# Row maxima on ScalarE's queue and GpSimd, both banks of the v sums copied at once, and low parts listed first

## The chip, the cores and the metric

One core of a Trainium2 chip runs the whole kernel. Its engines are TensorE (PE, with its weight loads shown apart as PEld), VectorE (DVE), ScalarE (ACT), GpSimd (POOL) and SyncE (SP), which in this kernel issues nearly all DMAs. The metric is the device time of one execution in microseconds. Before the change it is 772.84 us, the median of three runs (771.87 to 775.53).

## The reference

Two branches are computed from x (2048 rows of 512) and mixed by a gate:

```python
a  = x @ dft_hid_re.T ; b = x @ dft_hid_im.T
y  = dft_seq_re @ a - dft_seq_im @ b          # Fourier branch
q, k, v = split(x2 @ wqkv)                    # 32 heads of 16
p  = softmax(mask(q @ k.T / 4))               # keys i-255 .. i only
o  = (p @ v) @ wo                             # attention branch
g  = sigmoid(sum(x * gate_w))
out = g * y + (1 - g) * o
```

## The kernel before

**Precision.** Products that need it are made in two parts: an operand becomes a high part (a cast by `hi_of`, L103, on ACT) and a low part (raw minus high, `lo_of`, L106, on DVE or POOL), and three matmuls (high-high, high-low, low-high; `TERMS`) are summed.

**Attention.** 32 heads stand in eight groups of four, each with 16 blocks of 128 rows; the loop at the end of the program walks over the 128 blocks n. For a block, `s_head` (L442) multiplies queries by keys into a PSUM bank, and DVE (L445) finds each row's maximum into a column of `nm`, negated and masked. Nine blocks later (`LAG`), `t_head` (L497) makes the same scores transposed, with the maximum as two more rows of the contraction (the high and low part of it), and ACT takes the exponential (L498) into `pt`. POOL blanks the corners of the window (`t_mask`, L504 and L508). After four blocks `pv` (L523) multiplies `pt` by v into two banks `ot`, one for each half of the contraction.

**How the maxima get there.** Once per four blocks `m_rows` (L449) splits `nm` into two parts and transposes them on DVE (L452, L453, L455), writes them to DRAM (`m_scr<-mt`), and reads them back into rows 48 and 49 of `ring` (`ring<-m_scr`). Below such a round is called a batch; there are 33. `t_head` of three blocks later needs them.

**Banks.** The scores s, the transposed scores t and the two sums o take turns in four PSUM banks (`ps_a`, tag "st"). PE cannot start the next one before the oldest bank has been read: an s bank by DVE, a t bank by ACT, the o banks by ACT's copy (L529) and DVE's sum (L530).

**The other work.** `dense` is a generator of matmuls that the loop calls in between (`fill`): first the projections (to about 320 us), then 32 `c_block`s of the sequence DFT. Each of these takes a piece of the DFT matrix, loaded as `raw` and `big` tiles, split by `piece_split`: the high part, three plus or minus operations on the other quarters (L328, L331, on POOL twice and DVE once), the low part, and sums of magnitudes on ACT (L566), which a final guard adds up. When the loop is over, the rest of the `c_block`s and the output product (`wo_run`) follow.

**What sets the order.** Nothing schedules by itself: each engine runs its instructions in the order in which the program issues them, and waits in line. `defer(t, f)` issues f after t ticks; every matmul of `dense` is a tick, a step of the attention loop (one of the four heads of a block) is 0.7 and calls 2.8 of these matmuls in the first stretch and 1.25 in the second, and a `pv` is followed by `tick(9)` at once. So all that falls due in those nine ticks is issued just behind the `pv`. A DMA is issued by an engine too (`ld` takes SP), and an engine that must wait before it issues one holds up what stands behind it.

Of the kernel before, what the change touches and what calls it, by code (L numbers as in the profile page):

```python
# [8 lines left out]
F32 = mybir.dt.float32  # L9
# [41 lines left out]
def fnet_window_mix(ctx: ExitStack, tc: tile.TileContext, xT, x, wqk, wv, wr, wi, cr, ci, wo, gw, out):  # L51
# [44 lines left out]
    def ld(dst, src):  # L96
        nc.sync.dma_start(dst, src)  # L97

    def f(ap):
        return ap.bitcast(F32)  # L100
# [348 lines left out]
    def m_rows(u):  # L449
        m = ML.pop(u)  # L450
        hl = at.tile([P, 2, 16], F32R, name="mhl", bufs=1)
        nc.vector.tensor_scalar(hl[:, 0], m, -1.0, None, op0=OP.mult)  # L452
        nc.vector.scalar_tensor_tensor(hl[:, 1], m, -1.0, f(hl[:, 0]), op0=OP.mult, op1=OP.subtract)  # L453
        mt = at.tile([P, 32], F32, name="mt", bufs=1)
        nc.vector.transpose(mt, f(hl[:]).rearrange("q l c -> q (l c)"))  # L455
        ms = m_scr[u + LAG // 4 + 1]

        def write():
            ld(ms.rearrange("l h p b i q -> i (l h p b) q"), mt)
            defer(12, read)  # L460

        def read():
            b, end = max(0, LAG + 4 * u), min(NS * NB, LAG + 4 * u + 4)
            while b < end:
                e = min(end, (b // NB + 1) * NB)
                o = b - LAG - 4 * u
                for h in range(2):
                    ld(f(ring[0][64 * h + 48:64 * h + 50, :, b % NB * P:b % NB * P + (e - b) * P]),
                       ms[:, h, :, o:o + e - b].rearrange("l p b i q -> l p (b i q)"))
                b = e  # L470
        defer(2, write)

    PT = {}
    VR = {}
# [36 lines left out]
    def pv(u, last=False):  # L511
        g, sb = divmod(u, 4)
        ot = [ps_a.tile([P, 512], F32, name="o", tag="st") for _ in range(2)]
        kbs = range(max(0, 4 * sb - 2), 4 * sb + 4)
        for kb in kbs:
            pt = PT[g * NB + kb]
            v2 = V2[g * 4 + kb // 4][:, kb % 4]
            for j in range(NH):
                for h in range(2):
                    r = slice(64 * h, 64 * h + 64)  # L520
                    a = max(kb * P + (64 * h if kb else 0), sb * 512)
                    e = min(kb * P + 64 * h + 320, sb * 512 + 512)
                    nc.tensor.matmul(ot[h][32 * j:32 * j + 32, a - sb * 512:e - sb * 512], v2[r, j],  # L523
                                     pt[r, j, a - kb * P:e - kb * P], start=kb == kbs[0], stop=kb == kbs[-1],
                                     skip_group_check=True)
            if kb < 4 * sb + 2 or sb == 3:
                PT.pop(g * NB + kb)
        os = at.tile([P, 512], F32, name="os", bufs=1)
        nc.scalar.copy(os, ot[0])  # L529
        defer(3, lambda: nc.vector.tensor_add(os, ot[1], os))  # L530
        hf = g // 4
        us, ls = u_scr[sb][hf], l_scr[sb][hf]
        d = 40

        def o_out():
            ld(us[g % 4].rearrange("j r s -> (j r) s"), os)
            if g % 4 == 3:
                defer(d, o_pack)

        def o_pack():  # L540
            rows_ = us.rearrange("g j r s -> (g j) r s")
            ld(ls[0], rows_[:, 16])
            ld(o_scr[sb][2 * hf:2 * hf + 2].rearrange("a (b d) s -> (a b) d s", d=16), rows_[:, 0:16])
            defer(d, l_in)

        def l_in():
            lt = at.tile([P, 64], F32, name="lt")
            ld(lt, ls[0].rearrange("j (a b) -> (j a) b", b=64))
            defer(d, l_inv, lt)

        def l_inv(lt):
            nc.vector.reciprocal(lt, lt)
            defer(4, l_back, lt)

        def l_back(lt):
            ld(ls[1].rearrange("j (a b) -> (j a) b", b=64), lt)
            have.add(("o", sb, hf))
        defer(7, o_out)

    order = [(i, 4 * m + c) for i in range(2) for c in CLASSES for m in range(4)]  # L560
    PIECE = {}
# [31 lines left out]
    def piece_split(n, at_=1, step=2):  # L593
        if n >= len(order):
            return
        i, tb = order[n]
        raws = PRAW.pop(n)
        main = raws[0][:, HALVES[0]]
        hi = ev.tile([P, 512], F32R, name="es", bufs=3)
        w = st.tile([P, 2, 512], F32R, name="hl")  # L600
        defer(at_, hi_of, hi, main)
        for k, j in enumerate((2, 1, 3)):
            d, src, sign = left(i, tb, raws, j)
            defer(at_ + step * k, minus if sign > 0 else plus, d, d, src, j != 3)
        defer(at_ + step * 3, lo_of, w[:, 0], main, hi, True)
        for k, d in enumerate((raws[0][:, HALVES[1]], raws[1])):
            defer(at_ + step * (5 + k), magnitudes, sums[:, 2 * n + k:2 * n + k + 1], d, d)
        if n % 16 == 0:
            defer(at_ + step * 4, magnitudes, gl[:, i:i + 1], main, main)
        PIECE[i, tb] = hi, w[:, 0]  # L610
        if n == len(order) - 1:
            defer(at_ + step * 8 + 10, guard)
# [408 lines left out]
```

## Time and profile before

| | us |
|---|---|
| median of three runs | 772.84 |
| the profiled execution | 772.52 |
| its span on the core | 770.8 |
| end of the projections, by the loads of the DFT pieces | about 320 |
| last exponentials of the attention loop | about 664 |

The program keeps three stretches apart: projections beside attention up to about 320 us, `c_block`s beside attention up to about 680 us, and the tail of output products. The profile's busy times are those of one execution. A row of the waits names the engine, tile and line that waited, what it waited for, and then the total in us, the number of times and the longest. A row of the timeline has the start, the length, the engine, line and operation, the tiles, the shapes and, in brackets, the idle time before and what ended it.

### The profile page before, as it was taken

How to read it: one execution, taken by the hardware profiler on the slowest of the kernel's cores; microseconds unless marked ns; L12 is line 12 of the kernel's file. 1: busy time of each engine (PE TensorE's matmuls, PEld its weight loads, DVE VectorE, ACT ScalarE, POOL GpSimd, SP SyncE). 2: the span in 40 equal slices, each digit the busy share in tenths (PEclk: the TensorE clock that was granted, in tenths of full speed). 3: DMA queues.
4: the chain of work that ended last, by engine and by line, in shares of the span. 5: the costliest groups of instructions: out<-in, count | busy, mean ns of one | idle time of the engine just before them, and what ended most of it. 6: DMA issues, size and time to landing. Idle time of an engine off the chain costs nothing.

```text
span 770.8 us, 18841 instructions
## 1 busy us (share of the span) xinstructions
PE 650.1 (84%) x6558; PEld 499.8 (65%) x6558; DVE 544.1 (71%) x1471; ACT 437.8 (57%) x928; POOL 470.4 (61%) x718
## 2 busy tenths in 40 slices
PE   9999999899999999978677978878887687835976
PEld 6788887777788777766455655655555456624754
DVE  5388878898897889768567757676678863516554
ACT  6334775455576545666577657656756567514230
POOL 5002565667667878787768859796875869822000
PEclk9999999999999999989789879978978868975979
DMA  7857775777666877798868678885877648697675
GB/s 281 264 171 221 221 233 174 214 215 219 212 206 194 236 211 216 251 277 251 254 182 248 220 203 248 263 247 148 269 205 242 209 162 301 233 297 259 189 249 155
DMA packets 99994, 174.36 MB, mean 226 GB/s; under 512 B 34420, under 2 KB 35316, under 8 KB 99764
## 3 DMA queue, kind: packets, MB, share of 16 engines
q1 hardware_dynamic: 98452, 170.98, 72.2%
q10 hardware_dynamic: 1440, 2.10, 0.8%
q8 instruction: 54, 0.88, 0.5%
q14 instruction: 48, 0.39, 0.2%
HBM read 114.03 MB, written 63.46 MB: 230 GB/s over the span
## 4 chain that ended last, share of the span: by engine, by line
DMA 18%; PE 17%; POOL 8%; DVE 8%; issue 6%; SPq 4%; ACT 3%; DVEq 0%; POOLq 0%; ACTq 0%
DMA ring<-m_scr 5%; PE d L238 5%; SPq L97 4%; PE t L234 4%; DVE sm L445 3%; PE o L523 3%; DMA raw<-cr 3%; DMA ring<-qk_scr 3%; PE t L497 2%; DMA pt<-o_scr 2%; PE s L442 2%; POOL pt L504 1%; POOL hl L106 1%; DMA hl<-cr 1%; DMA ev<-wo 1%
## 5 line engine op out<-in xcount | busy, mean ns | idle before, releaser
L445 DVE CUSTOM_DVE_ANT_0 sm<-s,mask 128x384 f32<-128x384 f32 (+2 forms) x512 | 269.8, 527 | 87.0 <-PE s L442 41.9
L498 ACT ACTIVATE pt<-t 128x384 f32<-128x384 f32 (+2 forms) x512 | 234.2, 475 | 131.8 <-PE t L497 93.7
L497 PE MATMUL t<-ring,ring 50*128 50x384 f32 (+2 forms) x512 | 199.9, 400 | 56.6 <-DMA ring<-m_scr 32.0
L442 PE MATMUL s<-ring,ring 48*128 48x384 f32 (+2 forms) x512 | 185.0, 372 | 24.2 <-DVE nm L445 22.5
L504 POOL TENSOR_SCALAR_AFFINE_SELECT pt<-pt 128x256 f32<-128x256 f32 x256 | 116.0, 454 | 124.2 <-ACT pt L498 117.0
L238 PE MATMUL d<-big,hl 64*128 64x512 f32 x896 | 171.8, 421 | 0.0
L497 PEld LDWEIGHTS t<-ring,ring 50*128 50x128 f32 x512 | 101.9, 202 | 89.0 <-issue 26.5
L442 PEld LDWEIGHTS s<-ring,ring 48*128 48x128 f32 x512 | 99.4, 198 | 78.7 <-DVE nm L445 66.3
L238 PE MATMUL d<-hl,big 64*128 64x512 f32 x984 | 147.9, 395 | 0.0
L238 PE MATMUL d<-big,es 64*128 64x512 f32 x448 | 122.7, 473 | 0.0
L238 PEld LDWEIGHTS d<-big,hl 64*128 64x128 f32 x896 | 110.0, 198 | 5.2 <-issue 0.6
L238 PEld LDWEIGHTS d<-hl,big 64*128 64x128 f32 x984 | 105.2, 186 | 6.9 <-issue 0.8
L508 POOL TENSOR_SCALAR_AFFINE_SELECT pt<-pt 128x256 f32<-128x256 f32 x224 | 95.3, 425 | 0.0
L523 PE MATMUL o<-pt,vpad 64*32 64x320 f32 (+5 forms) x2816 | 83.3, 373 | 5.9 <-DVE nm L445 3.7
L523 PEld LDWEIGHTS o<-pt,vpad 64*32 64x32 f32 x2816 | 66.6, 113 | 28.1 <-DVE nm L445 10.3
L238 PEld LDWEIGHTS d<-big,es 64*128 64x128 f32 x448 | 66.3, 224 | 2.5 <-issue 0.6
L106 POOL TENSOR_TENSOR hl<-es,hl 128x512 fp32r<-128x512 f32 x14 | 19.0, 1359 | 65.2 <-ACT hl L103 61.6
L529 ACT COPY os<-o 128x512 f32<-128x512 f32 x32 | 18.8, 587 | 64.2 <-PE o L523 64.2
L530 DVE TENSOR_TENSOR os<-o,os 128x512 f32<-128x512 f32 x32 | 22.1, 690 | 42.8 <-ACT os L529 38.8
L106 POOL TENSOR_TENSOR hl<-raw,es 128x512 fp32r<-128x512 f32 x32 | 44.0, 1375 | 0.0
L243 ACT ACTIVATE es<-d 128x512 f32<-128x512 f32 x53 | 31.7, 598 | 19.8 <-PE d L238 19.0
L106 POOL TENSOR_TENSOR big<-big 128x512 fp32r<-128x512 f32 x32 | 41.6, 1304 | 0.2 <-ACT big L103 0.2
(100 smaller groups left out, 902.5 us busy)
## 6 DMA issues: line engine op xcount, KB each, us to landing
qk_scr<-hl SPq DMA_DIRECT2D x32, 512.0 KB
ring<-qk_scr SPq DMA_DIRECT2D x128, 128.0 KB
ring<-qk_scr SPq DMA_DIRECT2D x128, 64.0 KB
u_scr<-os SPq DMA_DIRECT2D x32, 256.0 KB
raw<-cr SPq DMA_DIRECT2D x16, 512.0 KB
big<-cr SPq DMA_DIRECT2D x16, 512.0 KB
raw<-ci SPq DMA_DIRECT2D x16, 512.0 KB
big<-ci SPq DMA_DIRECT2D x16, 512.0 KB
```

Of the source, the lines that this page charges most:

```text
L97: nc.sync.dma_start(dst, src)
L106: (nc.gpsimd if pool else nc.vector).tensor_sub(lo, raw, f(hi))
L234: nc.tensor.matmul(pss[0], w, x, start=start, stop=stop)
L238: nc.tensor.matmul(pss[h], w[r], x[r], start=start, stop=stop)
L243: nc.scalar.activation(t, pss[0], AF.Copy, scale=scale)
L442: nc.tensor.matmul(ps[:, :w], ring[0][r, p, jb * P:(jb + 1) * P], ring[1][r, p, k0:k0 + w], start=True, stop=True)
L445: nc.vector.tensor_tensor_reduce(out=sm[:, :w], in0=ps[:, :w], in1=mask[:, WIN - w:], scale=1.0, scalar=3e38, op0=OP.add, op1=OP.min, accu ...
L497: nc.tensor.matmul(ps[:, :w], ring[1][r, p, q0:q0 + P], ring[0][r, p, q0:q0 + w], start=True, stop=True)
L498: nc.scalar.activation(pt[:, j, :w], ps[:, :w], AF.Exp, scale=-1.0)
L504: nc.gpsimd.affine_select(a, a, pattern=[[0, 2], [1, P]], compare_op=OP.is_ge, fill=0.0, base=0, channel_multiplier=-1)
L508: nc.gpsimd.affine_select(a, a, pattern=[[0, 2], [-1, P]], compare_op=OP.is_gt, fill=0.0, base=0, channel_multiplier=1)
L523: nc.tensor.matmul(ot[h][32 * j:32 * j + 32, a - sb * 512:e - sb * 512], v2[r, j], pt[r, j, a - kb * P:e - kb * P], start=kb == kbs[0], st ...
```

## The change

Four things are edited.

1. `m_rows`: the split of the maxima goes from two DVE instructions to three POOL instructions; the transpose stays on DVE, two ticks later; the write to DRAM and the reads back are issued by ACT instead of SP. The write is due 4 ticks after the split (2 before), the read 9 ticks after the write (12 before).
2. `pv`: DVE copies the second bank into a tile `o1` (one of the three "es" buffers) at once, and the sum is made by POOL three ticks later. The store of the sum is due after 12 ticks (7 before).
3. `piece_split`: the high part goes to the unused half of the tile that holds the low part, instead of an "es" buffer.
4. `piece_split`: the low part is due one step after the high part (three before), and the plus and minus operations two steps later than before. The sums of magnitudes keep their place.

```diff
-        nc.vector.tensor_scalar(hl[:, 0], m, -1.0, None, op0=OP.mult)
-        nc.vector.scalar_tensor_tensor(hl[:, 1], m, -1.0, f(hl[:, 0]), op0=OP.mult, op1=OP.subtract)
+        nc.gpsimd.tensor_scalar(hl[:, 0], m, -1.0, None, op0=OP.mult)
+        nc.gpsimd.tensor_add(m, m, f(hl[:, 0]))
+        nc.gpsimd.tensor_scalar(hl[:, 1], m, -1.0, None, op0=OP.mult)
...
-        nc.vector.transpose(mt, f(hl[:]).rearrange("q l c -> q (l c)"))
+        defer(2, nc.vector.transpose, mt, f(hl[:]).rearrange("q l c -> q (l c)"))
...
-            ld(ms.rearrange("l h p b i q -> i (l h p b) q"), mt)
-            defer(12, read)
+            nc.scalar.dma_start(ms.rearrange("l h p b i q -> i (l h p b) q"), mt)
+            defer(9, read)
...
-                    ld(f(ring[0][64 * h + 48:64 * h + 50, ...]), ...)
+                    nc.scalar.dma_start(f(ring[0][64 * h + 48:64 * h + 50, ...]), ...)
...
-        defer(2, write)
+        defer(4, write)
...
+        o1 = ev.tile([P, 512], F32, name="es", bufs=3)
         nc.scalar.copy(os, ot[0])
-        defer(3, lambda: nc.vector.tensor_add(os, ot[1], os))
+        nc.vector.tensor_copy(o1, ot[1])
+        defer(3, lambda: nc.gpsimd.tensor_add(os, o1, os))
...
-        defer(7, o_out)
+        defer(12, o_out)
...
-        hi = ev.tile([P, 512], F32R, name="es", bufs=3)
         w = st.tile([P, 2, 512], F32R, name="hl")
+        hi = w[:, 1]
...
-            defer(at_ + step * k, minus if sign > 0 else plus, d, d, src, j != 3)
-        defer(at_ + step * 3, lo_of, w[:, 0], main, hi, True)
+            defer(at_ + step * (k + 2), minus if sign > 0 else plus, d, d, src, j != 3)
+        defer(at_ + step, lo_of, w[:, 0], main, hi, True)
```

Because of added lines, what was L498 is L499 in the changed kernel, L529 is L531, and L566 is L569.

**The read of one batch, on SP and ACT.** The batch is the one whose write is issued at 371 us in the profile before (`m_scr_172`). On SP before, its write stands behind eight loads of the rings and two copies in DRAM, and its read behind the loads of a DFT piece (`raw<-cr`, `big<-cr`):

```order
L97 DMA ring_281<-qk_scr_2_3_105 16x2x512
L97 DMA l_scr_0_194<-u_scr_0_202 16x512
L97 DMA o_scr_208<-u_scr_0_202 16x8192
L97 DMA m_scr_172<-mt 4x32x32
L97 DMA r_scr_0_210<-ev 128x512
L97 DMA raw<-cr 128x1024
L97 DMA big<-cr 128x1024
L97 DMA u_scr_0_204<-os 128x512
L97 DMA vr<-v_scr_111 128x4x64
L97 DMA l_scr_0_192<-lt 128x64
L97 DMA ring_280<-m_scr_172 2x2x512 x2
```

On ACT in the changed kernel, behind the copy of the first bank of the same `pv` (`pt<-t` are the exponentials, `raw,sums` and `big,sums` the sums of magnitudes):

```order
L531 COPY os<-o 128x512
L460 DMA m_scr_172<-mt 4x32x32
L103 CAST big<-big 128x512
L569 ACTIVATE raw,sums<-raw 128x512
L499 ACTIVATE pt<-t 128x384
L103 CAST big<-big 128x512
L569 ACTIVATE big,sums<-big 128x1024
L499 ACTIVATE pt<-t 128x384 x3
L103 CAST big<-big 128x512
L499 ACTIVATE pt<-t 128x384
L469 DMA ring_280<-m_scr_172 2x2x512 x2
L499 ACTIVATE pt<-t 128x384 x3
```

The write has left SP's line for a place right behind the copy, and the read stands five exponentials further on.

**The two banks, on DVE.** At the same `pv`, before: the split and the transpose, a plus or minus of a DFT piece, and the sum of the banks:

```order
L452 TENSOR_SCALAR mhl<-nm 128x16
L453 SCALAR_TENSOR_TENSOR mhl<-nm,mhl 128x16
L455 STREAM_TRANSPOSE mt<-mhl 128x32
L328 TENSOR_TENSOR big<-big,raw 128x512
L530 TENSOR_TENSOR os<-o,os 128x512
L445 ISA sm,nm<-s,mask 128x384
```

and in the changed kernel:

```order
L532 COPY es<-o 128x512
L94 STREAM_TRANSPOSE mt<-mhl 128x32
L328 TENSOR_TENSOR big<-big,raw 128x512
L445 ISA sm,nm<-s,mask 128x384
L445 ISA nm 128x1
```

The copy comes first, the transpose behind it, and two instructions are gone from DVE.

**The last pieces, on POOL.** The end of POOL's program, where only DFT pieces are left, before (`hl<-raw,es` is the low part, `raw<-raw` and `big<-big,hl` the plus and minus operations):

```order
L331 TENSOR_TENSOR raw<-raw 128x512
L328 TENSOR_TENSOR big<-big,hl 128x512
L106 TENSOR_TENSOR hl<-raw,es 128x512
L331 TENSOR_TENSOR raw<-raw 128x512
L328 TENSOR_TENSOR big<-big,hl 128x512
L106 TENSOR_TENSOR hl<-raw,es 128x512
L618 MEMSET gl 128x1
```

and in the changed kernel, with a sum of the two banks ahead of them:

```order
L533 TENSOR_TENSOR os<-es,os 128x512
L106 TENSOR_TENSOR hl<-raw,hl 128x512
L331 TENSOR_TENSOR raw<-raw 128x512
L328 TENSOR_TENSOR big<-big,hl 128x512
L106 TENSOR_TENSOR hl<-raw,hl 128x512
L331 TENSOR_TENSOR raw<-raw 128x512
L328 TENSOR_TENSOR big<-big,hl 128x512
```

Each piece's low part now stands ahead of the other two instead of behind them.

More of the change, by code (lines that the diff above doesn't have):

```diff
@@ L467, in read @@
                 for h in range(2):
-                    ld(f(ring[0][64 * h + 48:64 * h + 50, :, b % NB * P:b % NB * P + (e - b) * P]),
-                       ms[:, h, :, o:o + e - b].rearrange("l p b i q -> l p (b i q)"))
+                    nc.scalar.dma_start(f(ring[0][64 * h + 48:64 * h + 50, :, b % NB * P:b % NB * P + (e - b) * P]),
+                                        ms[:, h, :, o:o + e - b].rearrange("l p b i q -> l p (b i q)"))
                 b = e
-        defer(2, write)
+        defer(4, write)
     PT = {}
```

## The prediction

> **What bounds the kernel now.** First the busy times by stage, each row with its length, the busy us of PE, PEld, DVE, ACT and POOL, the granted PE clock and the DMA share:
>
> ```profile
> 40.00:320.00 280.00, 265.72 (x3121) 222.73 (x3117) 241.76 (x721) 163.56 (x341) 176.49 (x288) 1.00 0.69 210
> 320.00:680.00 360.00, 283.22 (x3049) 201.93 (x3049) 240.88 (x655) 230.60 (x524) 274.38 (x412) 0.85 0.77 234
> ```
>
> Up to 320 us PE is idle for only 14 us of 280. From 320 to 680 us it is idle for 77 of 360 and its clock falls to 0.85: there is room there. Second, PE's own waits in that second stretch:
>
> ```profile
> PE t L497 <- DMA ring<-m_scr: 32.0, 12, 7.0
> PE s L442 <- DVE nm L445: 14.2, 16, 3.7
> PE t L497 <- ACT pt L498: 10.0, 15, 2.1
> PE t L497 <- DVE os L530: 4.8, 14, 1.0
> ```
>
> Half of the idle time named is twelve waits for maxima read back from DRAM. The chain of work that ended last says the same, by line:
>
> ```profile
> DMA ring<-m_scr 5%; PE d L238 5%; SPq L97 4%; PE t L234 4%; DVE sm L445 3%; PE o L523 3%; DMA raw<-cr 3%; DMA ring<-qk_scr 3%; PE t L497 2%; DMA pt<-o_scr 2%; PE s L442 2%; POOL pt L504 1%; POOL hl L106 1%; DMA hl<-cr 1%; DMA ev<-wo 1%
> ```
>
> These reads are its largest share. Third, one of the waits, in the timeline:
>
> ```profile
> 362.75 6.30 SPq L97 DMA_DIRECT2D ring<-qk_scr  x8
> 364.70 0.21 DVE L455 STREAM_TRANSPOSE mt<-mhl 128x32 f32<-128x32 f32 x1
> 365.94 0.59 ACT L529 COPY os<-o 128x512 f32<-128x512 f32 x1 [1.14 <-PE o L523]
> 366.56 0.69 DVE L530 TENSOR_TENSOR os<-o,os 128x512 f32<-128x512 f32 x1
> 371.27 0.56 SPq L97 DMA_DIRECT2D m_scr<-mt  x1
> 375.52 0.63 SPq L97 DMA_DIRECT2D ring<-m_scr  x2
> 380.66 0.66 PE L497 MATMUL t<-ring,ring 50*128 50x384 f32 x1 [7.01 <-DMA ring<-m_scr]
> ```
>
> The transpose was done at 364.9, its write left SP at 371.27, 6.4 us later, behind eight ring loads. The read left at 375.52, and 4.5 us after its last issue (376.15) PE went on.
>
> **The change part by part.** The sum is made against the profiled execution, 772.52 us (span 770.8 and 1.7 around it), 0.3 under the median.
>
> *Maxima on ACT's queue (gain 24, bounds 16 and 32).* The write now stands behind ACT's copy: in the batch above it could leave at about 367 instead of 371.27. The read stands nine ticks behind `pv`, half of the 18 to the product that needs it. There `pv` ended at 365.8 and PE wanted the maxima at 373.65 (380.66 less 7.01). Half of these 7.8 us and 0.7 for the copy ahead give 4.6, so the read leaves at 370.4. How fast it lands on ACT's queue no row shows. The nearest two are SP's: 4.5 us above, and
>
> ```profile
> 331.12 0.59 SPq L97 DMA_DIRECT2D m_scr<-mt  x1
> 333.97 1.55 SPq L97 DMA_DIRECT2D ring<-m_scr  x4
> 336.75 0.66 PE L497 MATMUL t<-ring,ring 50*128 50x384 f32 x1 [4.44 <-DMA ring<-m_scr]
> ```
>
> 1.2 us (from 335.52). With 1.2 us all waits go (32). With 4.5 us the same sum leaves 1.3 us of the 7.0, and over twelve waits about 16. I take the middle, 24. The Trainium skill, DMA: Bandwidth & Descriptors, section Issuing engines are not separate DMA queues, says that DMAs of all issuing engines run on the same 16 engines and that a second issuer saves only its issuing time; by it the slow landing stays and this term is 16. The rows do not decide, as both landings are of one queue.
>
> *Both banks copied at once (gain 5, bounds 0 and 10).* In the timeline above the second bank was free at 367.25, 1.4 us after `pv`; a DVE copy that starts with ACT's frees it after about 0.7, taking it as long as ACT's:
>
> ```profile
> L529 ACT COPY os<-o 128x512 f32<-128x512 f32 x32 | 18.8, 587 | 64.2 <-PE o L523 64.2
> L530 DVE TENSOR_TENSOR os<-o,os 128x512 f32<-128x512 f32 x32 | 22.1, 690 | 42.8 <-ACT os L529 38.8 <-PE d L238 3.4 <-DMA big<-be_scr 0.3
> ```
>
> That is 0.7 us 32 times, 22 in all, but PE waits for this sum for just 4.8 (row above). The upper end adds the same again for maxima behind it.
>
> *The split leaves DVE (gain 4, bounds 0 and 8).*
>
> ```profile
> L453 DVE SCALAR_TENSOR_TENSOR mhl<-nm,mhl 128x16 fp32r<-128x16 f32 x33 | 17.8, 541 | 1.1
> L452 DVE TENSOR_SCALAR mhl<-nm 128x16 fp32r<-128x16 f32 x33 | 12.8, 386 | 0.0
> PE s L442 <- DVE nm L445: 8.4, 17, 1.0
> ```
>
> 33 splits cost DVE 30.6 us, yet inside `pv`, where it then idles for ACT's copy (38.8 above). What can be won is PE's wait for DVE in the first stretch (third row, 8.4); I take half.
>
> *ACT's new work (loss 6, bounds 0 and 25).*
>
> ```profile
> L97 SPq DMA_DIRECT2D ring<-m_scr x80: 225/254/1159, 45.7 to 643.3; - x80
> L97 SPq DMA_DIRECT2D m_scr<-mt x33: 514/532/1190, 42.6 to 637.1; - x33
> SPq L97 <- DMA m_scr<-mt: 18.6, 14, 3.2
> 268.22 0.53 SPq L97 DMA_DIRECT2D m_scr<-mt  x1
> 271.98 0.55 SPq L97 DMA_DIRECT2D ring<-m_scr  x2
> L498 ACT ACTIVATE pt<-t 128x384 f32<-128x384 f32 x448 | 214.1, 494 | 112.5 <-PE t L497 85.2 <-PE s L442 20.8 <-PE d L238 1.2
> ```
>
> The issues cost 33 x 0.53 + 80 x 0.25 = 37.5 us on ACT, busy 164 of 280 and 231 of 360. Worse is the wait for the write to land, which moves with the read: SP spent 18.6 us on it. A batch takes (637.1 - 42.6) / 32 = 18.6 us, a step (of 16) 1.16. In the first stretch a step is 3.5 ticks, so nine ticks are 3.0 us, and the read is due some 3.1 behind `pv`. The write leaves about 1.1 behind it (copy 0.7, transpose 0.2, gaps) and lands at most 3.8 later by the pair at 268.22, at most 2.9 by the pair at 331.12 above; with 3.2 it lands at 4.3. ACT then stands 1.2 us, 15 times, with all exponentials behind it. A t bank is wanted again after two steps, 2.3 us, of which the exponential takes 0.5 and the way to it and back as much or more, 1.2 in all. So of 1.2 us and 0.6 of issuing about 0.7 us a batch reaches PE: 11 us. DVE, the other bound there, catches up meanwhile, so I take about half.
>
> *POOL's new work (loss 8, bounds 0 and 25).*
>
> ```profile
> L106 POOL TENSOR_TENSOR hl<-raw,es 128x512 fp32r<-128x512 f32 x32 | 44.0, 1375 | 0.0
> L328 POOL TENSOR_TENSOR raw<-raw 128x512 f32<-128x512 f32 x16 | 20.9, 1304 | 4.4 <-DMA raw<-cr 4.2 <-POOL big L106 0.2
> L485 POOL COPY vpad<-vr 128x256 f32<-128x256 f32 x32 | 14.5, 453 | 0.0
> 420.00:440.00 20.00, 17.99 (x180) 11.47 (x177) 14.93 (x46) 13.09 (x34) 19.40 (x30) 0.91 0.68 210
> 460.00:480.00 20.00, 16.79 (x155) 10.99 (x152) 14.86 (x49) 16.10 (x38) 19.62 (x28) 0.97 0.76 229
> ```
>
> A sum of banks is like the second row, 1.3 us; a split of 16 columns is not shown, and lies between nothing and the third row's 0.45. I take 0.25. Each batch adds 1.3 + 3 x 0.25, about 2.1 us. The 17 batches of the second stretch add 35 to 274, so 310 of what is now 360. On the average that is hidden by POOL's idle time. In stretches like the two windows nothing hides it; with four such, 4 x 2.1 makes 8. If every batch were so, less what PE's removed waits gave POOL, it would be 25.
>
> *Low part first (gain 4 in the tail, bounds 0 and 7; loss 3 before it, bounds 0 and 10).*
>
> ```profile
> 696.03 0.62 ACT L103 CAST es<-raw 128x512 fp32r<-128x512 f32 x1 [9.26 <-DMA raw<-ci]
> 698.03 1.78 POOL L328 TENSOR_TENSOR big<-big,hl 128x512 f32<-128x512 f32 x1 [0.69 <-DMA hl<-cr]
> 699.77 1.71 POOL L106 TENSOR_TENSOR hl<-raw,es 128x512 fp32r<-128x512 f32 x1
> PE d L234 <- POOL hl L106: 3.3, 1, 3.3
> PE d L234 <- POOL gl L618: 3.6, 1, 3.6
> ```
>
> The last piece's low part ended at 701.5 behind two others, one waiting for a load. First in line it ends 1.3 us behind the cast, at 698.0: 3.5 us sooner, and PE's 3.6 us wait (put down to the next POOL instruction) goes. The 3.3 of the piece before is likely hidden, since the next raw load then ends the wait; 4 in all. Against it the plus and minus operations come four ticks later, and ACT's magnitudes, at their old place, wait for POOL:
>
> ```profile
> L566 ACT ACTIVATE big<-big 128x1024 f32<-128x1024 f32 x32 | 33.8, 1057 | 10.6 <-POOL pt L504 3.4 <-POOL big L328 3.1 <-POOL hl L106 2.3
> ```
>
> These 10.6 us may double; a third of that reaches PE. The high part's new place and the later store cost nothing: the one fills an unused half, the other has a whole batch (some 20 us) before its tile is wanted.
>
> *Sum:* -24 - 5 - 4 + 6 + 8 - 4 + 3 = -20, so 772.5 - 20 = **752.5 us**.
>
> **The rivals.**
> *Clock comes back.* In the second stretch the clock is 0.85. If it rises to 0.92 with the waits gone, 283 us of PE work shrink by 283 x (1 - 0.85/0.92) = 22, half of it on the path: 752.5 - 11 = 741, and with all 32 us of the first term 733. For it: the first stretch has little idle time and a clock of 1.00. Against it: other waits stay. The Trainium skill, TensorE: Matmul & The Clock Gate, Part 1, has the clock halve after an idle window of about 3.4 us; by it only the waits of 4.4 and 7.0 us above must cost clock, and a wait of 1 us need not.
>
> *The next transfer is late instead.*
>
> ```profile
> 378.66 0.62 ACT L103 CAST es<-raw 128x512 fp32r<-128x512 f32 x1 [4.59 <-DMA raw<-cr]
> ```
>
> In the longest wait ACT's cast waited for a DFT piece until 378.66, 2 us before PE went on. If pieces or ring loads set the pace (DMA share 0.77), or reads on ACT land as slowly and stand behind such a cast, two thirds of the 24 us go: 768.
>
> *The other side: ACT stands still.* All exponentials, casts and evictions stand behind the reads. If in the first stretch's 15 batches the 1.2 us and 0.6 of issuing reach PE in full, and in the other 18 the issuing alone, that is 27 + 11 = 38 in place of 6: 752.5 + 32 = 784.5. It decides from about 0.8 us a batch on: 33 x 0.8 = 26 eats the other terms (-37 + 11). For it: only two t banks, and 3.1 against 4.3 us. Against it: in the second stretch a step is 1.95 ticks, nine ticks are 5.3 us, more than the write needs, and ACT is idle for over a third of both stretches.
>
> **How the numbers follow.** A measurement of this kernel tells about 0.5% from no change, 769.0 to 776.7. The forecast (742 to 762) gets 0.45, the clock 0.17, the late transfer 0.20 (half of it under 769), ACT or POOL on the other side 0.18 (0.03 within, 0.15 over). Faster 0.45 + 0.17 + 0.10 = 0.72, same 0.13, slower 0.15. The range runs from 731 to 781: it leaves out about 0.06 below and 0.12 above.
>
> **What would show it right or wrong.** PE's waits for ring<-m_scr should fall from 32 to about 8 us and those for the sum of banks to nearly none. ACT should show waits for m_scr<-mt ahead of its reads, some 1 us each before 320 us and few later. POOL should be near 510 us busy and the low part of the last piece about 3.5 us earlier against its cast. The prediction is wrong if the reads leave ACT later than 6 us behind `pv`, if PE's waits for exponentials (10.0) grow by over 15 us, or if the first stretch grows by over 10.

## The result, and the profile after

| | before | changed |
|---|---|---|
| median, us (4 runs each) | 774.18 | 831.09 |
| lowest to highest | 771.87 to 785.91 | 829.21 to 835.21 |
| ratio, 95% interval | | 1.0753 (1.0692 to 1.0814) |
| span of the profiled execution | 770.8 | 827.5 |
| first load of a DFT piece leaves SP | 319.9 | 336.6 |
| last transposed product ends | 664.3 | 721.8 |

The change makes the kernel 7.5% slower, where 2.6% faster was forecast. Medians and ranges here and below are of all executions, while the ratios leave out those that fell into the device's slower state. The three stretches say where: the first grew by 16.7 us, the second by 721.8 - 336.6 - (664.3 - 319.9) = 40.8, and the tail shrank by 0.8.

First the busy times by stage of the changed kernel, with its own limits of the stretches (columns as before the change: length, busy us of PE, PEld, DVE, ACT and POOL, clock, DMA share):

```profile
40.00:340.00 300.00, 272.86 (x3149) 224.99 (x3152) 228.72 (x685) 162.80 (x345) 206.24 (x348) 0.99 0.65 198
340.00:740.00 400.00, 305.04 (x3038) 222.48 (x3016) 225.65 (x622) 231.61 (x521) 310.03 (x480) 0.78 0.69 211
740.00:828.00 88.00, 61.82 (x230) 46.03 (x230) 46.30 (x63) 23.03 (x28) 8.42 (x7) 0.81 0.74 224
```

Two things stand in the second row. PE's idle time is 400 - 305 = 95 us where it was 77, and about as many matmuls (3038 and 3049) keep PE busy 305 us in place of 283, at a clock of 0.78 in place of 0.85. About half of this stretch's loss is waiting, and half is the matmuls themselves running slower. ACT is busy for 232 of 400 us, no more than before: nothing in its busy time tells that it is late. The waits do. PE's own in that stretch:

```profile
PE t L498 <- ACT pt L499: 37.9, 28, 5.2
PE s L442 <- DVE nm L445: 26.7, 26, 3.8
PE s L442 <- ACT pt L499: 10.4, 6, 6.5
PE t L498 <- DMA ring<-m_scr: 3.8, 3, 1.7
```

The wait for maxima, 32.0 us before, is 3.8: that part did what it says. In its place PE waits for exponentials, 37.9 us where it was 10.0, for an s bank behind an exponential, 10.4 where it was 0.2, and for DVE's maxima, 26.7 where it was 14.2. In the first stretch the wait for exponentials is new:

```profile
PE t L498 <- ACT pt L499: 11.6, 13, 2.0
```

Why the exponentials are late shows in the timeline of one batch, here ACT's rows, then two of SP's and one of PE's:

```profile
475.39 0.58 ACT L531 COPY os<-o 128x512 f32<-128x512 f32 x1 [1.17 <-PE o L524]
478.01 0.51 ACTq L460 DMA_DIRECT2D m_scr<-mt  x1
478.57 0.49 ACT L499 ACTIVATE pt<-t 128x384 f32<-128x384 f32 x1 [2.59 <-DVE nm L445]
...
480.77 0.94 ACT L499 ACTIVATE pt<-t 128x384 f32<-128x384 f32 x2
485.18 0.83 ACTq L469 DMA_DIRECT2D ring<-m_scr  x2
486.05 0.87 ACT L499 ACTIVATE pt<-t 128x384 f32<-128x384 f32 x2 [4.34 <-DMA big<-a_scr]
```

```profile
471.36 5.99 SPq L97 DMA_DIRECT2D ring<-qk_scr  x8
...
479.62 0.91 SPq L97 DMA_DIRECT2D big<-a_scr  x2
```

```profile
486.59 0.68 PE L498 MATMUL t<-ring,ring 50*128 50x384 f32 x1 [3.35 <-ACT pt L499]
```

ACT stands for 2.6 us around the write and for 4.3 around the reads, and PE then waits 3.35 us for an exponential. The end of the second stand is put down to `big<-a_scr`, a load on SP that the maxima have nothing to do with. The program's list of instructions, with the counters that each waits for, tells why (SP's rows, then ACT's, of this batch; DVE_49 and Pool_49 are counters of the engines' own work):

```
L97 DMA vr<-v_scr_111 128x4x64 [waits DMAHW1_49,Pool_49]
L97 DMA u_scr_1_205<-os 128x512 [waits DMAHW3_49,Pool_49]
L97 DMA big<-a_scr_142 128x512 [waits DMAHW4_49]
L97 DMA big<-a_scr_143 128x512 [waits DMAHW5_49]
L97 DMA r_scr_14_224<-ev 128x512 [waits DMAHW6_49,DVE_49]
...
L460 DMA m_scr_176<-mt 4x32x32 [waits DMAHW2_49,DVE_49]
L469 DMA ring_280<-m_scr_176 2x2x512 [waits DMAHW4_49,DMAHW2_49]
L469 DMA ring_280<-m_scr_176 2x2x512 [waits DMAHW5_49]
```

The DMAs of SP and ACT take eight completion counters (DMAHW0 to 7) in turn, in the order of the program, and each waits until the DMA that had its counter before, the eighth before it, has landed. SP's rows skip number 2: ACT's write has it. ACT's first read waits for its own data (2) and for counter 4, and the second for counter 5, which `big<-a_scr_142` and `_143` had. The counters' times in the trace agree. The maxima had landed at 480.64, counter 4 was full at 485.10, and the first read left at 485.18; counter 5 was full at 485.75, and the second read left at 485.77. The write was held in the same way: its transpose was done at 476.25, but counter 2 (a ring load of SP's) was full only at 477.94, and the write left at 478.01; the row's `DVE nm L445` is no cause there. So an engine that issues a DMA in this program also waits for SP's line, however early its own data is there.

Adding up, for every issue of ACT, the time from the end of its instruction ahead to the issue, and putting it to the counter that rose last: ACT issued for 39 us, stood 38 us for its own data (the transpose or the landed write) and 32 us for shared counters, 109 us in all. Not every microsecond of standing is lost, as ACT may have had nothing to do in some of them; the experiments price it.

POOL's new work and what waits for it:

```profile
L533 POOL TENSOR_TENSOR os<-es,os 128x512 f32<-128x512 f32 x32 | 43.3, 1355 | 27.4 <-ACT os L531 21.3 <-DMA hl<-cr 2.2 <-issue 1.7
L452 POOL TENSOR_SCALAR mhl<-nm 128x16 fp32r<-128x16 f32 x33 | 10.4, 315 | 33.1 <-DVE nm L445 33.1
L454 POOL TENSOR_SCALAR mhl<-nm 128x16 fp32r<-128x16 f32 x33 | 8.6, 262 | 2.9
L453 POOL TENSOR_TENSOR nm<-nm,mhl 128x16 f32<-128x16 f32 x33 | 7.8, 237 | 2.7
DVE mt L94 <- POOL mhl L454: 24.4, 15, 3.9
SPq L97 <- POOL os L533: 53.0, 20, 12.2
```

A split costs POOL 315 + 237 + 262 ns, a sum of banks 1355 ns, about as assumed. But the split stands in POOL's line, and DVE, which needs it for the transpose, stood for it 24.4 us. SP, which stores the sum of the banks, stood 53.0 us for POOL (last row).

The sums of magnitudes on ACT, and the last DFT piece (ACT's cast, PE, POOL, PE):

```profile
L569 ACT ACTIVATE raw<-raw 128x512 f32<-128x512 f32 x34 | 21.4, 628 | 29.0 <-POOL raw L331 15.4 <-POOL big L328 6.5 <-POOL raw L328 4.3
L569 ACT ACTIVATE big<-big 128x1024 f32<-128x1024 f32 x32 | 33.8, 1055 | 18.6 <-POOL big L331 4.1 <-POOL big L328 3.8 <-POOL pt L509 3.4
```

```profile
754.33 0.62 ACT L103 CAST hl<-raw 128x512 fp32r<-128x512 f32 x1 [8.79 <-DMA raw<-ci]
755.00 1.22 PE L234 MATMUL d<-big,hl 128*128 128x512 f32 x2 [9.77 <-ACT hl L103]
755.08 1.27 POOL L106 TENSOR_TENSOR hl<-raw,hl 128x512 fp32r<-128x512 f32 x1 [10.72 <-ACT hl L103]
756.41 4.63 PE L234 MATMUL d<-big,hl 128*128 128x512 f32 x10 [0.19 <-POOL hl L106]
PE d L234 <- ACT hl L103: 17.1, 2, 9.8
```

The low part ends 1.4 us behind the end of the cast (756.35 against 754.95), where it was 4.8, and PE's waits of 3.3 and 3.6 us for it are down to 0.19. But PE then waits longer for the cast (17.1 us for two, 12.4 before), which waits for a load.

### The profile page after: what moved, and what is told of

It is laid out like the page before. It is cut to its first block, busy times and chain, and to the rows that moved or that the text cites. A ratio compares the mean times of both kernels' runs of the same rounds, so it can differ in the third digit from the quotient of the medians.

```text
span 827.5 us, 18851 instructions
## 1 busy us (share of the span) xinstructions
PE 678.5 (82%) x6558; PEld 522.7 (63%) x6558; DVE 517.1 (62%) x1405; ACT 437.3 (53%) x928; POOL 535.8 (65%) x849
## 4 chain that ended last, share of the span: by engine, by line
DMA 17%; PE 14%; POOL 12%; DVE 6%; ACT 5%; issue 4%; SPq 2%; ACTq 0%; DVEq 0%; POOLq 0%
PE d L238 6%; DMA ring<-qk_scr 3%; PE t L498 3%; PE o L524 2%; SPq L97 2%; PE s L442 2%; DMA pt<-o_scr 2%; ACT pt L499 2%; DMA rl<-l_scr 2%; POOL big L331 2%; DVE sm L445 2%; DMA big<-cr 2%; ACT big L569 2%; POOL pt L505 1%; POOL big L106 1%
## 5 line engine op out<-in xcount | busy, mean ns | idle before, releaser
L445 DVE CUSTOM_DVE_ANT_0 sm<-s,mask 128x384 f32<-128x384 f32 (+2 forms) x512 | 270.7, 529 | 107.8 <-PE s L442 59.3
L499 ACT ACTIVATE pt<-t 128x384 f32<-128x384 f32 (+2 forms) x512 | 230.6, 471 | 143.1 <-PE t L498 51.1
L238 PE MATMUL d<-big,hl 64*128 64x512 f32 x1344 | 298.0, 465 | 0.5 <-DVE es L246 0.5
L498 PE MATMUL t<-ring,ring 50*128 50x384 f32 (+2 forms) x512 | 211.0, 422 | 66.9 <-ACT pt L499 49.5
L442 PE MATMUL s<-ring,ring 48*128 48x384 f32 (+2 forms) x512 | 195.2, 391 | 43.6 <-DVE nm L445 31.8
L238 PEld LDWEIGHTS d<-big,hl 64*128 64x128 f32 x1344 | 184.9, 223 | 10.7 <-issue 2.0
L498 PEld LDWEIGHTS t<-ring,ring 50*128 50x128 f32 x512 | 109.3, 216 | 101.4 <-ACT pt L499 71.2
L106 POOL TENSOR_TENSOR hl<-raw,hl 128x512 fp32r<-128x512 f32 x39 | 50.0, 1281 | 26.9 <-ACT hl L103 26.6
L533 POOL TENSOR_TENSOR os<-es,os 128x512 f32<-128x512 f32 x32 | 43.3, 1355 | 27.4 <-ACT os L531 21.3
L532 DVE COPY es<-o 128x512 f32<-128x512 f32 x32 | 22.0, 686 | 59.9 <-PE o L524 59.9
L531 ACT COPY os<-o 128x512 f32<-128x512 f32 x32 | 18.8, 587 | 62.8 <-PE o L524 59.7
L569 ACT ACTIVATE big<-big 128x1024 f32<-128x1024 f32 x32 | 33.8, 1055 | 18.6 <-POOL big L331 4.1
L246 DVE SCALAR_TENSOR_TENSOR es<-d,es 128x512 f32<-128x512 f32 x53 | 36.4, 687 | 11.4 <-ACT es L243 11.2
L445 DVE DVE_READ_ACCUMULATOR2_ANT nm<- 128x1 f32 x512 | 42.3, 83 | 0.1
```

Source lines behind the costliest of these rows:

```text
L106: (nc.gpsimd if pool else nc.vector).tensor_sub(lo, raw, f(hi))
L238: nc.tensor.matmul(pss[h], w[r], x[r], start=start, stop=stop)
L246: nc.vector.scalar_tensor_tensor(t, pss[1], scale, t, op0=OP.mult, op1=OP.add)
L442: nc.tensor.matmul(ps[:, :w], ring[0][r, p, jb * P:(jb + 1) * P], ring[1][r, p, k0:k0 + w], start=True, stop=True)
L445: nc.vector.tensor_tensor_reduce(out=sm[:, :w], in0=ps[:, :w], in1=mask[:, WIN - w:], scale=1.0, scalar=3e38, op0=OP.add, op1=OP.min, accu ...
L498: nc.tensor.matmul(ps[:, :w], ring[1][r, p, q0:q0 + P], ring[0][r, p, q0:q0 + w], start=True, stop=True)
```

## The experiments

All ratios are against the kernel before on the same chip, with 95% intervals.

### Each part alone

`a_split` is the kernel before with POOL's split and the later transpose, the DMAs still on SP.

```diff
-        nc.vector.tensor_scalar(hl[:, 0], m, -1.0, None, op0=OP.mult)
...
+        nc.gpsimd.tensor_scalar(hl[:, 0], m, -1.0, None, op0=OP.mult)
...
+        defer(2, nc.vector.transpose, mt, f(hl[:]).rearrange("q l c -> q (l c)"))
```

> The kernel before with one part of the change alone: the split of the maxima on POOL (three instructions) and the transpose two ticks later; SP still issues the write and the reads. Theory P (POOL is late, and whoever waits for it in line loses): DVE stands before the transpose some 20 us in total, PE's waits for DVE's maxima grow, and the time is 10 to 20 us over before. Theory Q (ACT stands at the DMAs it now issues): within 4 us of before. Theory L (the new order of the DFT pieces makes ACT wait for POOL's plus and minus operations): within 4 us of before.

`a_queue` has only the maxima's DMAs on ACT, with the change's ticks.

```diff
-            ld(ms.rearrange("l h p b i q -> i (l h p b) q"), mt)
-            defer(12, read)
+            nc.scalar.dma_start(ms.rearrange("l h p b i q -> i (l h p b) q"), mt)
+            defer(9, read)
...
-                    ld(f(ring[0][64 * h + 48:64 * h + 50, ...]), ...)
+                    nc.scalar.dma_start(f(ring[0][64 * h + 48:64 * h + 50, ...]), ...)
...
-        defer(2, write)
+        defer(4, write)
```

> The kernel before with one part alone: the write of the maxima and the reads back issued by ACT, due 4 and 9 ticks later as in the changed kernel; the split stays on DVE. Theory Q: PE's waits for exponentials grow by 20 us or more and the time is 15 to 35 us over before. Theory P: the waits for the reads go (32 us to under 6) and nothing takes their place, so 10 to 25 us under before. Theory L: as P.

`a_bank` has only DVE's copy of the second bank, POOL's sum and the later store.

```diff
+        o1 = ev.tile([P, 512], F32, name="es", bufs=3)
...
-        defer(3, lambda: nc.vector.tensor_add(os, ot[1], os))
+        nc.vector.tensor_copy(o1, ot[1])
+        defer(3, lambda: nc.gpsimd.tensor_add(os, o1, os))
...
-        defer(7, o_out)
+        defer(12, o_out)
```

> The kernel before with one part alone: both banks of the sums of v copied at once, the sum on POOL, its store due after 12 ticks. Theory P: 32 sums of 1.36 us make POOL late and SP stands behind the store, 10 to 25 us over before. Theory Q and theory L: 0 to 8 us under before, since the second bank comes free 0.7 us sooner.

`a_low` has only the new order of the pieces, with the high part in its new place.

```diff
-        hi = ev.tile([P, 512], F32R, name="es", bufs=3)
...
+        hi = w[:, 1]
...
-            defer(at_ + step * k, minus if sign > 0 else plus, d, d, src, j != 3)
-        defer(at_ + step * 3, lo_of, w[:, 0], main, hi, True)
+            defer(at_ + step * (k + 2), minus if sign > 0 else plus, d, d, src, j != 3)
+        defer(at_ + step, lo_of, w[:, 0], main, hi, True)
```

> The kernel before with one part alone: the low part of a DFT piece listed first, plus and minus operations two steps later, the high part in the other half of the low part's tile. Theory L: ACT's waits for POOL ahead of the magnitudes grow from 14 to 40 us or more, PE's waits for exponentials by 15, and the time is 10 to 25 us over before. Theory P and theory Q: 0 to 5 us under before, by the tail.

Measured, and beside it the same part undone in the changed kernel:

| part | alone, us | ratio | undone, us | ratio |
|---|---|---|---|---|
| split | 782.35 | 1.0115 (1.0027 to 1.0202) | 825.53 | 1.0644 (1.0572 to 1.0716) |
| queue | 802.92 | 1.0306 (1.0187 to 1.0426) | 799.05 | 1.0291 (1.0208 to 1.0374) |
| banks | 785.39 | 1.0167 (1.0068 to 1.0266) | 814.81 | 1.0545 (1.0470 to 1.0619) |
| low part | 781.42 | 1.0089 (1.0046 to 1.0132) | 825.72 | 1.0650 (1.0572 to 1.0728) |

Every part alone is slower, the low part by little more than this kernel's own half per cent of scatter. Against the 774.16 of these runs the medians are 8.2, 28.8, 11.2 and 7.3 us over, 55.5 together, close to the 57 of the whole; by the ratios it is 9, 24, 13 and 7 us. The queue is about half of it. Four views, of `a_queue`, of `a_split`, of `a_low` and of `a_bank`:

```profile
PE t L497 <- ACT pt L498: 36.6, 33, 7.3
PE t L497 <- DMA ring<-m_scr: 6.3, 3, 2.5
```

```profile
DVE mt L94 <- POOL mhl L454: 52.0, 24, 5.1
```

```profile
ACT raw L566 <- POOL raw L331: 14.0, 8, 3.2
```

```profile
PE s L442 <- DVE nm L445: 35.9, 41, 5.8
```

With the queue alone the waits for maxima fall from 32.0 to 6.3 us, and those for exponentials rise from 10.0 to 36.6. The first stretch grew by 13.5 us and the second by 14.6, although 25.7 us of waits in the second were gone. With the split alone DVE stands for POOL for 52.0 us, to save 30.6 of its own work; PE's waits for DVE's maxima, which were expected to grow, stayed (22.7 us, 22.5 before), and those for DVE's sum of the banks grew from 4.8 to 16.2. With the new order ACT's sums wait 14.0 us for POOL's operations, where this row was 2.0. That is less than was expected, and PE's waits for exponentials hardly moved (11.4 us); those for DVE's maxima grew from 22.5 to 33.4, so how this part costs its time is not shown. The banks are no plainer: PE's waits for the sum are gone, those of s for DVE are 35.9 us (22.5 before) and those for exponentials 15.6; which of copy, POOL's sum and later store does it was not taken apart.

### Each part undone

The reverse of these diffs, one part at a time, in the changed kernel.

> The changed kernel with the split of the maxima and the transpose put back on DVE as before; ACT still issues the DMAs. The changed kernel is 57 us over before. Theory P: the 24 us of DVE's waits before the transpose go, 15 to 25 us under the changed kernel. Theory Q and theory L: within 5 us of the changed kernel.

> The changed kernel with the write and the reads issued by SP again, at the ticks of before. Theory Q: ACT's idle time around the reads (50 us) goes, 20 to 40 us under the changed kernel. Theory P: SP stands 53 us behind POOL's sums of banks, so the reads come later still, and the time is equal or up to 15 us over the changed kernel. Theory L: within 10 us.

> The changed kernel with the sum of the two banks on DVE as before, its store after 7 ticks. Theory P: 15 to 30 us under the changed kernel, with SP's 53 us of waiting for the sum gone. Theory Q and theory L: within 8 us.

> The changed kernel with the pieces of the DFT matrix split in the old order, and the high part in its old buffer. Theory L: ACT's waits for POOL ahead of the magnitudes fall from 48 to about 14 us, and the time is 15 to 30 us under the changed kernel. Theory P: about 5 to 10 us under it, as less waits on a late POOL. Theory Q: within 4 us.

The table above has the times: 5.6, 32.0, 16.3 and 5.4 us under 831.09. The intervals of split and low part overlap that of the whole change, so only queue and banks are each shown this way. Split and low part were expected to give back 15 us or more each by the theories that blamed POOL and the new order.

### Which DMA, and when

`w_act` has the write on ACT (4 ticks) and the reads on SP (9 ticks behind); `r_act` has the write on SP and the reads on ACT, both at their old ticks; `q_late` is `a_queue` with the reads 12 ticks behind the write.

```diff
-            defer(9, read)
+            defer(12, read)
```

> The kernel before with the write of the maxima on ACT 4 ticks after the split, and the reads on SP 9 ticks after the write. Q-issue: 0.53 of the 1.02 us a batch is left, so +5 to +12 beside the gain of earlier reads: 770 to 785. Q-wait: the wait for landing moves to SP, ACT keeps only the wait for the transpose (33 us of idle time around the writes with both on ACT): 772 to 785. Q-order: half of SP's relief, 780 to 795. PE's waits for maxima should be near 15 us by all three.

> The kernel before with the reads of the maxima on ACT and the write on SP as before (2 and 12 ticks). Q-issue: 0.5 us a batch, +5 to +12: 775 to 790. Q-wait: the write leaves SP late (371.27 where the read was due at about 370), so ACT stands for SP's line and the landing both, the worst of the three: 795 to 815, with ACT idle for 60 us or more ahead of its reads. Q-order: 775 to 785.

> Write and reads of the maxima on ACT as in the change, but the reads 12 ticks behind the write in place of 9 (in the first stretch about 1 us later, in the second about 1.8). Q-issue: no better than with 9 ticks (802.9), as the issues are the same: 797 to 808. Q-wait: ACT's standing ahead of the reads (23.9 and 20.6 us with 9 ticks) falls to under 15 in all, and the time to 775 to 792. Q-order: 797 to 808.

Measured: 778.99, ratio 1.0048 (1.0004 to 1.0092); 803.67, 1.0361 (1.0282 to 1.0439); 799.39, 1.0280 (1.0207 to 1.0353). The reads cost far more than the write. ACT stood 22 us ahead of its issues in `w_act`, 52 in `r_act` (43 of it for its own data) and 37 in `q_late`, which was expected under 15 in all: twelve ticks take only some 9 of `a_queue`'s 46 us of standing away, and the time hardly changes.

### What a standing ACT costs

`dummy` leaves the maxima on SP and adds, at the change's places on ACT, a write and two copies a batch that nobody needs and that wait for no data.

```diff
+            nc.scalar.dma_start(dm.rearrange("l h p b i q -> i (l h p b) q"), mask[:, :32])
+            defer(9, dummy_read)
...
+                nc.scalar.dma_start(dr[h], x[h, 0:4].rearrange("(a c) s -> a c s", a=2))
```

> The kernel before with the maxima's write and reads left on SP, and beside them, at the places where the change puts them on ACT, DMAs of the same sizes that wait for nothing and that nobody needs (a write of mask columns to DRAM, two copies of 8 KB inside DRAM). They add to the work and do not replace any. Theory Q-issue (ACT's issuing itself, about 1 us a batch, puts the exponentials late): +15 to +30 us, 789 to 804, with PE's waits for exponentials in the second stretch up from 10 to 25 or more. Theory Q-wait (what costs is that ACT waits for the transpose and for the write to land): +0 to +8, 774 to 782. Theory Q-order (relieving SP moves the other transfers): +0 to +6, since SP's line is what it was.

Measured: 830.72, 1.0692 (1.0604 to 1.0779), beyond all three expectations. ACT's timeline of one batch:

```profile
489.37 0.49 ACT L511 ACTIVATE pt<-t 128x384 f32<-128x384 f32 x1 [0.70 <-PE s L445]
492.35 2.14 ACTq L482 DMA_DIRECT2D r_dum<-x  x2
494.54 0.87 ACT L511 ACTIVATE pt<-t 128x384 f32<-128x384 f32 x2 [4.68 <-DMA big<-a_scr]
```

The first copy reads an input, so nothing but its counter can hold it, and ACT still stands until an SP load has landed. Summed as above: 56 us issuing (0.58 a write, 0.50 a copy), 78 us for shared counters, none for data. The counters bind SP too: it stood 6.2 us for the landing of ACT's writes.

Four runs then part standing from DMAs. `delay1` and `delay3` put copies of 64 columns (0.245 us each) on ACT near the change's places, 4 and 13 a batch; the second lot is due 13 ticks behind the split, some ticks ahead of the change's reads, and in 14 batches, most of them in the first stretch, all thirteen run in a row. `spread` has the 13 one tick apart; `dummy_sp` has the DMAs of `dummy` issued by SP. The first diff is that of `delay3` (2 and 2 copies in `delay1`), the second that of `spread`.

```diff
+        defer(4, stand, 4)
+        defer(13, stand, 9)
```

```diff
+        for k in range(13):
+            defer(10 + k, stand, 1)
```

> The kernel before, with small copies on ScalarE that nobody needs, two where the change puts the write of a batch and two where it puts its reads: about 1 us a batch (33 us in all), the issuing time of the change without a DMA. Theory Standing (each us in which ScalarE stands at these places costs 0.3 to 0.5 us of the end): +8 to +18 us, 783 to 793. Theory Issuing free (short stops are caught up; only waits of several us cost): +0 to +5, 775 to 780. Theory Traffic (the DMAs themselves cost): +0 to +5.

> The same with four and nine copies, about 3.2 us a batch (107 us in all), which is what ScalarE stood in the changed kernel by its trace (39 issuing, 37 for its own data, 32 for the shared counters). Standing: +35 to +60 us, 810 to 836, PE's waits for exponentials over 60 us. Issuing free: +30 to +60 as well, since these are stops of over 1 and 2 us. Traffic: +0 to +15.

> The thirteen unneeded copies a batch of delay3, but each due a tick after the one before, from ten ticks behind the split on, so that one or two stand between two exponentials in place of four and nine (or thirteen) in a row. Sum of the time lost counts: as slow as delay3, 820 to 840. Length of a stop counts: stops of 0.25 to 0.5 us are caught up, 774 to 790.

> The kernel before with the DMAs of the run dummy (a write and two copies a batch that nobody needs) issued by SP in place of ScalarE, at the same ticks. Standing: most of the 54 us is gone, as ScalarE stands nowhere; SP's line is longer by 1.6 us a batch, so +3 to +18, 779 to 794. Traffic: as slow as dummy, 815 to 835.

| run | on ACT | us | ratio |
|---|---|---|---|
| delay1 | 132 copies, in stops of 0.5 to 1.1 us, 35 us in all | 773.28 | 0.9949 (0.9903 to 0.9995) |
| delay3 | 429 copies, in stops of 1.1 to 3.6 us, 117 us in all | 835.14 | 1.0736 (1.0604 to 1.0868) |
| spread | 429 copies, nearly all one to four at a time (0.2 to 1.1 us), 111 us in all | 789.60 | 1.0243 (1.0172 to 1.0314) |
| dummy_sp | none, DMAs on SP | 796.43 | 1.0251 (1.0175 to 1.0327) |

PE's waits for exponentials in `delay1`, `delay3` and `spread`:

```profile
PE t L503 <- ACT pt L504: 11.8, 17, 2.2
```

```profile
PE t L503 <- ACT pt L504: 41.6, 36, 4.1
```

```profile
PE t L503 <- ACT pt L504: 20.8, 36, 2.2
```

About the issuing time of the change (39 us), as copies, costs nothing that these runs show. About the whole time that ACT issued and stood in the changed kernel costs 57 us by the ratio, in stops without any DMA, and as many copies cut into stops of nearly always 0.2 to 1.1 us cost 19. So the length of a stop counts more than the sum, which keeps a smaller part; `spread` also moved the stops to other ticks, and place and length were not taken apart. The extra DMAs without a standing ACT cost 19 us by the ratio, a little more than expected; PE then waits 46.8 us for maxima (32.0 before), whose line on SP is longer. So DMAs as such explain at most that much of `dummy`'s 54.

### Other places for the maxima

`q_pool` is `a_queue` with the DMAs issued by POOL, which has counters of its own. `sp_early` is the kernel before with the write and reads moved forward in SP's line:

```diff
-            defer(12, read)
+            defer(16, read)
...
-        defer(2, write)
+        write()
```

The read is then due seven ticks behind the `pv` in place of twelve.

> The kernel before with the maxima's write (4 ticks) and reads (9 ticks behind it) issued by GpSimd, whose DMAs have counters of their own. Standing: ScalarE stands nowhere and the maxima leave SP's line, so PE's waits for them fall as in the change, but GpSimd stands for the write to land as ScalarE did (25 us) and pays for issuing: 765 to 785. Traffic, or that SP's relief itself moves other transfers to worse places: 790 to 805, as with ScalarE's queue.

> The kernel before with the maxima's write due at once (2 ticks before) and the reads four to five ticks nearer to it in SP's line, ahead of the loads of a DFT piece in several batches; ScalarE and GpSimd issue nothing. If the read's place in SP's line is what PE waits for, the waits for maxima fall from 32 to 15 to 25 us and the time to 762 to 772. If another transfer is late in its place, within 0.5% of before: 770 to 778. If SP itself stands for the write to land and delays the pieces, 778 to 790.

Measured: `q_pool` 831.87, 1.0616 (1.0510 to 1.0723), beyond both expectations. POOL now stands:

```profile
POOL m_scr L459 <- DVE mt L455: 45.7, 9, 29.8
POOL ring L468 <- DMA m_scr<-mt: 43.2, 21, 4.8
PE t L497 <- DMA ring<-m_scr: 37.8, 17, 6.7
```

(29.8 of the first row lie at the start.) The reads wait on POOL for the write to land, the masks stand behind them, and PE still waits 37.8 us for maxima. `sp_early`: 770.00, 0.9943 (0.9896 to 0.9990), the waits for maxima down from 32.0 to 19.3 us: 12.7 us of waits are worth about 4 us of time. Its interval lies under 1, but so does that of `delay1` (0.9949), which only adds useless work, so half a per cent is no gain that these runs show. No version clearly beats the kernel before.

## Why the prediction was wrong, point by point

**Maxima on ACT's queue, -24: the waits went, the gain did not.** Alone they fell by 25.7 us, inside the bounds of 16 and 32, but the kernel lost 24 to 29. PE only waited for something else. `sp_early` says the same without any new engine: a microsecond of these waits is not a microsecond of time. The lower bound was also worked out too high: it leaves out the 0.6 us that the two reads take to issue, with which 1.9 us a wait would stay and the gain be about 9. The Trainium skill, DMA: Bandwidth & Descriptors, section Issuing engines are not separate DMA queues, says that a second issuer saves only sequencer time; by it this term was 16. The trace has more of the waits gone (25.7 us), yet agrees with its drift, that another issuer gives little.

**ACT's new work, +6: the step that failed.** The queue alone cost 24 us by the ratio and 29 by the medians, net of whatever the 25.7 us of waits that went were worth: some 50 in all if they were worth as much, 24 if they were worth nothing, against 6. The sizes of the issues were right (39 us against 37.5), and as much in copies costs nothing (`delay1`). Wrong was the wait: 1.2 us a batch, for the write to land, in the first stretch only. That wait came as said, about 16 us in the changed kernel against 15 times 1.2. But ACT stood 70 us ahead of its issues: the other 54 were 32 for SP's DMAs through the shared counters, which the prediction didn't look at, 16 ahead of the writes for transposes, some of which POOL made late, and 6 for landed writes in the second stretch. With the queue alone it stood 46 (26 for data and 20 for counters). "In the second stretch nine ticks are more than the write needs" was nearly right for the landing and beside the point: there the stands were mostly of the other kinds. For the first stretch the working had 11 us before it was halved, and `a_queue` has 13.5; the second, which the 6 left out, lost 14.6 on top of whatever its 25.7 us of waits were worth. The slack of about 1.2 us behind two t banks was a fair guess: `delay3`'s stops of up to 3.6 us in the first stretch put its end from 319.9 to 348.2, 1.9 us a batch, so about 1.6 were caught up.

**The split leaves DVE, -4.** Alone +8.2. Its 30.6 us do leave DVE, but DVE waits 52.0 us for POOL's line. The sum had POOL's busy time, not the wait of DVE, which needs the result at once.

**POOL's new work, +8.** Busy time rose by 65 us (470.4 to 535.8), as its own 2.1 us a batch give; the 510 named as a sign did not follow from them. The price was mis-sized: split and banks, which hold this work, cost 8.2 and 11.2 us alone, where the three terms together had -1. It was worked out from windows in which POOL is full, while 0.8 us behind a piece of 1.3 us can be late anywhere, as DVE's 52.0 us show for the split.

**Both banks at once, -5.** PE's wait for the sum is gone as said (4.8), but alone the part costs 11.2. The cause stays open beyond this: PE waits longer for DVE's maxima and ACT's exponentials.

**Low part first, -4 and +3.** The low part came 3.4 us sooner behind its cast (3.5 forecast) and both waits went, but PE's wait for the cast grew from 12.4 to 17.1 us, and the tail gained 0.8 (nothing in `a_low`, 106.5 us before and after). The load of the piece was late next, which the prediction allowed for on one of the two pieces only. Before the tail, ACT's idle time ahead of the sums of magnitudes grew by 33.6 us in the whole change (14.0 to 47.6, both rows), where the 10.6 of one row was assumed to double; alone the part costs 7.3.

**The rivals.** "ACT stands still" was right in kind, at 0.18 together with POOL: all three signs of being wrong came, the waits for exponentials up by 27.9 us (15 was the mark), the first stretch longer by 16.7 (10), and reads later than 6 us behind `pv` in 14 of the second stretch's 17 batches. Its price, 38 us and 784.5, fell short of the queue's, and it counted no stands but issuing in the second stretch. "The next transfer is late" was not it for the queue: in `a_queue`'s second stretch ACT's casts waited for no DFT piece (5.0 us before). "Clock comes back" went the other way: 0.85 fell to 0.78. The Trainium skill, TensorE: Matmul & The Clock Gate, Part 1, has the clock halve after an idle window of about 3.4 us. The trace's clock record has the clock at half in 19 pieces (106 us) of the second stretch before and in 28 (173 us) after, while PE had four idle times over 3.4 us in both; those of 1 to 3.4 us went from 18 (29 us) to 27 (46 us). So most halvings came without such a long idle time, and that shorter waits need not cost clock, as the prediction read the rule, is not borne out.

## What to carry to other kernels

Before a DMA is moved to a compute engine, read in the program's list which counters its issue waits for, and who raised them last: in this program the engine then waited for SP's DMAs too. Price a stand by its length against the slack of the buffers behind that engine, not by its share of the engine's time. A short step that another engine needs at once can lose on an engine whose line is made of long ones, as the split did here.

## What the runs showed that was not expected

- In these runs ACT lost 35 us in stops of 0.5 to 1.1 us at no cost; 117 us in stops of 1.1 to 3.6 cost 57, and 111 in stops of nearly always 1.1 or less 19.
- POOL did its three operations of 128x16 in 237 to 315 ns each (814 in all), where DVE's two took 386 and 541 (927).
- A DMA issue took ACT 0.23 us (median) for a read and 0.52 for the write, and POOL 0.56 and 0.72.
- The granted clock of the second stretch fell from 0.85 to 0.78 with no more idle times of PE over 3.4 us than before (four), but more of 1 to 3.4.
